# One-token attention with a cached K and V: K scored on TensorE from a transposed layout, V multiplied and summed in one VectorE pass

## The chip, the cores and the metric

The kernel runs on one NeuronCore of one Trainium2 chip. A core has five engines with a program each: TensorE for matmuls (PE in the profile, its weight loads PEld), VectorE (DVE), ScalarE (ACT), GpSimd (POOL) and SyncE (SP). They meet through semaphores. Data comes from HBM into SBUF (128 partitions) by 16 DMA engines; a transfer is issued from an engine's queue, here mostly SP's, and the transfers of one queue start in order. TensorE writes into PSUM.

The metric is the device time of one execution in microseconds (us). A profiled execution also gives the span from its first to its last instruction.

## The reference, cut to what matters

```python
B, Sq, D = 1, 1, 640                      # one token
H, Sk, Dh = 32, 8192, 192                 # 32 heads, 8192 cached positions; all float32
q = (layernorm(x) @ wq) per head
scores = einsum("bhqd,bhkd->bhqk", q, k_cache) * Dh ** -0.5
p = softmax(scores)
o = einsum("bhqk,bhkd->bhqd", p, v_cache)
h = x + o.reshape(B, Sq, H * Dh) @ wo
n = layernorm(h)
gate, up = n @ W_gate, n @ W_up           # 640 -> 1536
h2 = h + (gate * (gate > 0) * up) @ W_down
```

K and V of one head are 6.29 MB each. All heads together are 402.7 MB, `wq` and `wo` 15.7 MB each, the three FFN matrices 11.8 MB: 445.9 MB read once.

## The kernel before, in words

Every big tile lives in the pool `kv`, three slots of 128 x 12,288 floats. `load_kv` (L77) brings one head of K or V as it lies in HBM: partition p holds 64 consecutive positions of 192 numbers. All loads are issued on SP's queue; a load waits until its slot is free.

At the start the whole of `wq` comes through the same three slots, and 60 matmuls (L160) make the queries of all heads at once, 8 heads in each group of 32 partitions. `query(h)` (L168) then copies two heads' queries to all 128 partitions with one selecting matmul (L173).

The K side of a head is `head_step` (L181): DVE multiplies a quarter of the tile by the query (L188), POOL adds its upper half onto the lower (L189), and three DVE sums (L193) leave the scores as 128 x 64. `softmax_steps` (L196) takes the maximum over all scores (a DVE maximum, a TensorE transpose, a second maximum), the exponential with its sum on ACT, a matmul with ones for the total, and scales.

The V side is `values_of` (L234). Of the 64 positions of a partition, 40 go through TensorE two at a time (`pairs`, L226), 12 are scaled on ACT (L240) and 12 on DVE (L241); POOL folds the products together (L246). `finish_steps` (L289) sums over partitions with small matmuls (L299), transposes, and after each group of heads multiplies by that group's rows of `wo`, loaded by `load_wo` (L86). The last two heads use TensorE alone (`values_last`).

The loop (L325) interleaves heads: in turn h it loads K of head h+1 and V of head h, and the softmax of head h and the finishing of head h-1 are generators that `head_step(h+1)` advances between its quarters. A planner orders the rest; `keep` pins single instructions to program order.

After the loop the FFN weights come through two of the same slots (L359 to L363), `h4` takes the attention result from PSUM (L368), a layer norm follows (L370 to L386), and up, gate and down are multiplied on TensorE (L392, L409) with the residual added at L412.

Of the kernel before, what the change touches and what calls it, by code (L numbers as in the profile page):

```python
# [11 lines left out]


@with_exitstack
def kernel(
# [3 lines left out]
    kc: bass.AP,  # L19
    vc: bass.AP,  # L20
    wq: bass.AP,
    wo: bass.AP,
# [6 lines left out]
    P, Q, NQ = 128, 32, 4  # L29
    _, H, S, DH = kc.shape  # L30
    D = wq.shape[0]
    F = w_gate.shape[1]
    DJ = D // P
    R = 32
    NCH = S // (P * R)
    NS = S // P
    SUB = 16
    TW = R * DH
    HPQ = H // NQ
    QB = 512  # L40
    NQB = HPQ * DH // QB
    DG = D // NQ
    FG = F // NQ
    FJ = F // P
    SCALE = DH ** -0.5
    EPS = 1e-5
    GROUPS = [list(range(4 * i, 4 * i + 4)) for i in range(7)] + [[28, 29], [30, 31]]
    group_of = {h: (gi, i) for gi, hs in enumerate(GROUPS) for i, h in enumerate(hs)}

    kf, vf = kc[0], vc[0]  # L50
# [3 lines left out]
    wts = ctx.enter_context(tc.tile_pool(name="wts", bufs=2))  # L54
    small = ctx.enter_context(tc.tile_pool(name="small", bufs=2))
    row = ctx.enter_context(tc.tile_pool(name="row", bufs=1))
    ps_q = ctx.enter_context(tc.tile_pool(name="ps_q", bufs=2, space=bass.MemoryType.PSUM))
    ps_x = ctx.enter_context(tc.tile_pool(name="ps_x", bufs=1, space=bass.MemoryType.PSUM))
    ps_o = ctx.enter_context(tc.tile_pool(name="ps_o", bufs=1, space=bass.MemoryType.PSUM))
    ps_s = ctx.enter_context(tc.tile_pool(name="ps_s", bufs=2, space=bass.MemoryType.PSUM))  # L60
# [3 lines left out]
    xrow = const.tile([1, D], F32, name="xrow")  # L64
    nc.scalar.dma_start(xT, x[0, 0].rearrange("(p j) -> p j", p=P))
    nc.scalar.dma_start(xrow, x[0])


    wq_v = wq.rearrange("(p j) n -> p j n", p=P)
    wq_ts = []  # L70
    for j in range(0, DJ, 2):
        n = min(2, DJ - j)
        t3 = kv.tile([P, 2 * TW], F32, name="kv_t").rearrange("p (j n) -> p j n", n=TW)[:, 0:n, :]
        nc.sync.dma_start(t3, wq_v[:, j:j + n, :])
        wq_ts += [t3[:, i, :] for i in range(n)]

    def load_kv(src, h, parts):  # L77
        t = kv.tile([P, 2 * TW], F32, name="kv_t")
        v = src[h].rearrange("(p r) d -> p (r d)", p=P)
        b = 0  # L80
        for n in parts:
            nc.sync.dma_start(t[:, b:b + n], v[:, b:b + n])  # L82
            b += n
        return t

    def load_wo(gi):  # L86
        hs = GROUPS[gi]
        j = len(hs) * DH // P
        t = wts.tile([P, j, D], F32, tag="wo_t", name="wo_t")
        r0 = hs[0] * DH  # L90
        nc.sync.dma_start(t, wo[r0:r0 + len(hs) * DH, :].rearrange("(p j) n -> p j n", p=P))
        return t

    ones = const.tile([P, P], F32, name="ones")
    nc.gpsimd.memset(ones, 1.0)
    eps = const.tile([P, 1], F32, name="eps")
# [5 lines left out]
    sel = const.tile([P, NQ, P], F32, name="sel")  # L102
    nc.gpsimd.memset(sel, 0.0)
    for g in range(NQ):
        nc.gpsimd.memset(sel[g * Q:g * Q + 1, g, :], 1.0)

    par = const.tile([P, 2, Q], F32, name="par")
    for i in range(2):
        nc.vector.reduce_sum(par[:, i, 0:1], ident.rearrange("p (g c) -> p g c", c=Q)[:, :, i], axis=AX.X)
        nc.vector.tensor_copy(par[:, i, 1:Q], par[:, i, 0:1].to_broadcast([P, Q - 1]))  # L110
# [14 lines left out]

    s1 = const.tile([P, 1], F32, name="s1")
    nc.vector.reduce_sum(s1, xT, axis=AX.X)  # L127
    pm = ps_s.tile([P, 512], F32, name="ps_small")
# [9 lines left out]
    pv = ps_s.tile([P, 512], F32, name="ps_small")  # L138
# [7 lines left out]


    acc = ps_a.tile([P, DG], F32, name="acc")
    for g in range(NQ):
        nc.tensor.matmul(acc[g * Q:(g + 1) * Q, :], ones[0:1, 0:Q], xrow[:, g * DG:(g + 1) * DG],  # L150
                         start=True, stop=False)


    qps = [ps_q.tile([P, QB], F32, tag="q", name=f"qp{b}") for b in range(2)]
    qps.append(ps_x.tile([P, QB], F32, tag="x", name="qp2"))
    for j in range(DJ):
        for b in range(NQB):
            for g in range(NQ):
                c0 = g * HPQ * DH + b * QB
                nc.tensor.matmul(qps[b][g * Q:(g + 1) * Q, :], xn[:, j:j + 1].to_broadcast([P, Q]),  # L160
                                 wq_ts[j][:, c0:c0 + QB], start=(j == 0), stop=(j == DJ - 1))
    q4 = const.tile([P, HPQ * DH], F32, name="q4")
    for b in range(NQB):
        nc.scalar.mul(q4[:, b * QB:(b + 1) * QB], qps[b], SCALE)  # L164

    pair_of = {}

    def query(h):  # L168

        g, i = divmod(h, HPQ)  # L170
        if i % 2 == 0:
            q = ps_q.tile([P, QB], F32, tag="q", name="q")
            nc.tensor.matmul(q[:, 0:2 * DH], sel[:, g, :], q4[:, i * DH:(i + 2) * DH], start=True, stop=True)  # L173
            pair_of[h // 2] = q
        return pair_of[h // 2][:, (i % 2) * DH:(i % 2 + 1) * DH]
# [166 lines left out]
    for _ in done:  # L342
        pass
# [97 lines left out]
```

## Time and profile before

| | |
|---|---|
| median of 3 runs | 1044.49 us (1044.29 to 1044.98) |
| profiled execution | span 1042.8 us, 5875 instructions |
| moved by DMA | 446.28 MB, mean 428 GB/s |
| mean granted TensorE clock | 0.621 |
| TensorE clock by slice | between 0.5 and 0.9 |

How to read it: the profile lists for each engine its busy time and its share of the span; for groups of instructions (source line, engine, operation, shapes, count) the busy time of the group, the mean time of one in ns, and the idle time in front of them with what ended most of it. `SPq` or `ACTq` is an engine's sequencer, which issues transfers. The chain is the work that ended last, followed back from the last instruction. In the timeline the first two numbers are start and length in us, and a row can merge several like instructions (`x24`); for a float32 matmul two passes are recorded, so `x24` with four column groups are three steps of the sum. In the view by stretches the columns are length, busy time and count of PE, PEld, DVE, ACT and POOL, then the granted TensorE clock as a share, the share of the DMA engines, and GB/s.

### The profile page before, as it was taken

Reading aid. Unit: us, or ns where it says so; the run is one execution under the profiler, and the core shown is the slowest. Engines: PE = TensorE matmul, PEld = TensorE weight load, DVE = VectorE, ACT = ScalarE, POOL = GpSimd, SP = SyncE. Lnnn points to the kernel's source line nnn. Section 1 sums busy time; section 2 is a strip of 40 time slices with the busy share of each in tenths; the row PEclk is TensorE's granted clock in tenths of the full one; section 3 lists DMA queues with packets and bytes.
Section 4 is the critical chain, followed back from the end, with each engine's and each line's share of the span. In section 5 each row is a group of like instructions: output and inputs, shape, how many; then the busy total and the mean of one; then the engine's idle time right before and its main releaser. Section 6 shows DMA issues by size and latency. Waiting matters only on the chain.

```text
span 1042.8 us, 5875 instructions
## 1 busy us (share of the span) xinstructions
PE 311.4 (30%) x2056; PEld 91.5 (9%) x2056; DVE 779.6 (75%) x445; ACT 161.8 (16%) x471; POOL 776.5 (74%) x321
## 2 busy tenths in 40 slices
PE   1603232222234212232322222242222323230376
PEld 0100000000000000000000000000000000010122
DVE  1087988688888888688986888788886889878641
ACT  0101111011111101111110111111111111110110
POOL 0057888788887888688897888868886888888730
PEclk9955655665656556566666656565565665565577
DMA  9999999999999999999999999999999999999997
GB/s 392 446 430 432 425 441 426 437 427 436 432 434 430 428 438 424 439 425 440 432 432 430 434 432 430 433 432 434 430 423 441 436 432 430 432 436 424 433 423 307
DMA packets 12998, 446.28 MB, mean 428 GB/s; under 512 B 1573, under 2 KB 1577, under 8 KB 3114
## 3 DMA queue, kind: packets, MB, share of 16 engines
q1 hardware_dynamic: 12824, 445.92, 99.3%
q8 instruction: 16, 0.26, 0.1%
q14 instruction: 12, 0.10, 0.0%
q10 hardware_dynamic: 146, 0.01, 0.0%
HBM read 445.91 MB, written 0.00 MB: 428 GB/s over the span
## 4 chain that ended last, share of the span: by engine, by line
DMA 77%; DVE 14%; PE 5%; POOL 3%; issue 1%; ACT 0%; SPq 0%; ACTq 0%; POOLq 0%; DVEq 0%
DMA kv_t<-in_A_k_cache_dram 70%; DVE kv_t L188 12%; DMA ffn_b<-in_B_W_down_dram 3%; PE ps_small L299 2%; DMA kv_t<-in_A_v_cache_dram 2%; DMA xrow<-in_A_x_dram 2%; POOL kv_t L246 2%; PE ps_small L200 1%; POOL kv_t L189 1%; DVE sc L193 1%; PE qp L160 1%; DVE kv_t L241 1%; DVE mp L198 0%; PE pd L409 0%; SPq L82 0%
## 5 line engine op out<-in xcount | busy, mean ns | idle before, releaser
L188 DVE TENSOR_TENSOR kv_t<-kv_t,q 128x3072 f32<-128x3072 f32 x128 | 427.4, 3342 | 182.8 <-DMA kv_t<-in_A_k_cache_dram 182.4
L189 POOL TENSOR_TENSOR kv_t<-kv_t 128x1536 f32<-128x1536 f32 x128 | 438.2, 3448 | 96.1 <-DVE kv_t L188 85.1
L246 POOL TENSOR_TENSOR kv_t<-kv_t 128x1152 f32<-128x1152 f32 (+1 forms) x180 | 337.2, 1874 | 125.7 <-DVE kv_t L241 80.7
L193 DVE TENSOR_REDUCE sc<-kv_t 128x16 f32<-128x1536 f32 (+1 forms) x96 | 213.2, 2273 | 0.7 <-POOL kv_t L189 0.7
L230 PE MATMUL po<-kv_t,pn 128*2 128x384 f32 x1328 | 162.0, 653 | 104.1 <-DMA kv_t<-in_A_v_cache_dram 104.1
L200 PE MATMUL ps_small<-ident,mp 128*128 128x128 f32 x32 | 14.2, 444 | 449.0 <-DVE mp L198 449.0
L240 ACT ACTIVATE kv_t<-kv_t,pn 128x192 f32<-128x192 f32 x360 | 127.8, 441 | 101.9 <-DMA kv_t<-in_A_v_cache_dram 98.4
L241 DVE TENSOR_TENSOR kv_t<-kv_t,pn 128x2304 f32<-128x2304 f32 x30 | 103.3, 3444 | 0.0
L206 ACT ACTIVATE p<-sc,m 128x64 f32<-128x64 f32 x32 | 11.1, 348 | 583.7 <-DVE m L203 583.7
L230 PEld LDWEIGHTS po<-kv_t,pn 128*2 128x2 f32 x1328 | 38.1, 103 | 219.1 <-issue 219.1
L200 PEld LDWEIGHTS ps_small<-ident,mp 128*128 128x128 f32 x32 | 5.8, 180 | 471.7 <-issue 426.9
L276 PE MATMUL acc<-wo_t,oT 128*3 128x480 f32 x112 | 32.8, 898 | 18.0 <-DVE oT L303 18.0
L173 PE MATMUL q<-q,sel 128*128 128x384 f32 x32 | 20.7, 747 | 56.9 <-DVE kv_t L188 56.9
L208 PE MATMUL ps_small<-rs,ones 128*128 128x1 f32 x64 | 18.6, 359 | 59.7 <-ACT p L206 59.7
L213 ACT ACTIVATE pn<-p,rl 128x64 f32<-128x64 f32 x32 | 11.1, 348 | 102.7 <-DVE rl L212 102.7
L299 PE MATMUL ps_small<-kv_t,ones 128*32 128x192 f32 (+1 forms) x64 | 24.8, 508 | 2.2 <-POOL kv_t L246 2.2
L208 PEld LDWEIGHTS ps_small<-rs,ones 128*128 128x128 f32 x64 | 15.8, 307 | 86.2 <-ACT p L206 74.5
L303 DVE STREAM_TRANSPOSE oT<-ps_small 32x192 f32<-32x192 f32 (+1 forms) x32 | 11.7, 364 | 10.2 <-PE ps_small L299 9.5
L160 PE MATMUL qp<-kv_t,xn 128*32 128x512 f32 x120 | 17.2, 737 | 5.5 <-DMA kv_t<-in_A_wq_dram 3.1
L242 DVE TENSOR_TENSOR kv_t<-po,par 128x384 f32<-128x384 f32 x30 | 16.3, 544 | 0.0
L268 DVE MEMSET acc<- 128x512 f32 x1 | 0.5, 485 | 20.9 <-ACT q L164 20.9
L127 DVE TENSOR_REDUCE s<-xT 128x1 f32<-128x5 f32 x1 | 0.2, 157 | 17.1 <-DMA xT<-in_A_x_dram 17.1
(82 smaller groups left out, 102.7 us busy)
## 6 DMA issues: line engine op xcount, KB each, us to landing
kv_t<-in_A_k_cache_dram SPq DMA_DIRECT2D x32, 6144.0 KB, 24.1
kv_t<-in_A_v_cache_dram SPq DMA_DIRECT2D x31, 6144.0 KB, 23.2
wo_t<-in_A_wo_dram SPq DMA_DIRECT2D x7, 1920.0 KB, 27.1
kv_t<-in_A_wq_dram SPq DMA_DIRECT2D x2, 6144.0 KB, 17.8
ffn_a<-in_B_W_up_dram SPq DMA_DIRECT2D x1, 3840.0 KB
kv_t<-in_A_wq_dram SPq DMA_DIRECT2D x1, 3072.0 KB, 40.0
kv_t<-in_A_v_cache_dram SPq DMA_DIRECT2D x1, 3072.0 KB, 17.2
kv_t<-in_A_v_cache_dram SPq DMA_DIRECT2D x4, 768.0 KB, 20.8
```

Source lines behind the costliest of these rows:

```text
L160: nc.tensor.matmul(qps[b][g * Q:(g + 1) * Q, :], xn[:, j:j + 1].to_broadcast([P, Q]), wq_ts[j][:, c0:c0 + QB], start=(j == 0), stop=(j == ...
L188: keep(nc.vector.tensor_mul(ks, ks, q[:, None, :].to_broadcast([P, SUB, DH])))
L189: nc.gpsimd.tensor_add(ks[:, :, 0:HD], ks[:, :, 0:HD], ks[:, :, HD:DH])
L193: keep(nc.vector.reduce_sum(sc[:, i0:i1], k3[:, i0:i1, 0:HD], axis=AX.X))
L200: keep(nc.tensor.transpose(pt[:, 0:P], mp.to_broadcast([P, P]), ident))
L208: nc.tensor.matmul(pl[:, 0:1], ones, rs, start=True, stop=True)
L230: nc.tensor.matmul(po[g * Q:g * Q + 2, :], pn[:, 2 * i:2 * i + 2], vt[:, 2 * i * DH:(2 * i + 2) * DH], start=(i < NQ), stop=(i >= n - NQ))
L240: nc.scalar.activation(v3[:, r, :], v3[:, r, :], AF.Copy, scale=pn[:, r:r + 1])
L241: keep(nc.vector.tensor_mul(v3[:, RV:NS, :], v3[:, RV:NS, :], pn[:, RV:NS, None].to_broadcast([P, RN, DH])))
L246: nc.gpsimd.tensor_add(v3[:, r:r + n, :], v3[:, r:r + n, :], v3[:, s:s + n, :])
L276: nc.tensor.matmul(acc3[g * Q:g * Q + 3, 0:W3], oT[:, t:t + 3, 0], w3[:, g * W3:(g + 1) * W3], start=(gi == 0 and t == 0), stop=(gi == LAS ...
L299: nc.tensor.matmul(pt[q0:q0 + Q, 0:W], par[:, k, :] if n > 1 else ones[:, 0:Q], ob[:, k * DH + u * W:k * DH + (u + 1) * W], start=(k == 0) ...
```

## The change

The host now packs two arrays, one row of 128 x 13,248 floats for each head. In `kq` K is transposed, so that the 192 dimensions of a head run over partitions: 128 of them in columns 0 to 8,191, the other 64 in two halves in the next 4,096; behind them lie that head's columns of `wq`, 960 floats a partition. In `vo` V is transposed as well: partition 16 g + c holds, for position group g, the dimensions c, c + 16, ..., each as 1,024 consecutive positions; behind them lie that head's rows of `wo`. Two loads serve one head, and the pool `kv` has three slots of 128 x 13,248.

For each head `query` makes the query from the tile's own `wq` columns, five matmuls that leave it on all 128 partitions. `columns` turns it into columns over partitions (two short DVE multiply-and-sums with an identity, two ACT scalings with masks). `scores` is 24 matmuls of 512 columns into a 128 x 1,024 PSUM tile, where a group of 16 partitions carries the same 1,024 scores, followed by the softmax on that tile. `values` is 12 DVE passes over 128 x 1,024, each multiplying a slice of V by the probabilities and summing along the row into one column, then a matmul that adds the position groups, and two short sums that divide by the softmax total. `output` adds the head's product with `wo` to `acc` with three matmuls.

The kernel runs in the written order on each engine (`manual_schedule`): query of the next head stands between values and output of this one on TensorE. POOL only fills constants. The last V tile comes in four pieces. `x` in columns moves from ACT's queue to the front of SP's; `h4` is read from PSUM in four pieces of 32 partitions; the first two loads of `W_down` are joined. The layer norms and the FFN are as before.

```diff
-    def head_step(q, kt, *works):
-        sc = small.tile([P, NS], F32, name="sc")
-        k3 = kt.rearrange("p (r d) -> p r d", d=DH)
-        parts = [(i0, k3[:, i0:i0 + SUB, :]) for i0 in range(0, NS, SUB)]
-        for i0, ks in parts:
-            keep(nc.vector.tensor_mul(ks, ks, q[:, None, :].to_broadcast([P, SUB, DH])))
-            nc.gpsimd.tensor_add(ks[:, :, 0:HD], ks[:, :, 0:HD], ks[:, :, HD:DH])
...
+    ctx.enter_context(tc.manual_schedule())
+    xT = const.tile([P, DJ], F32, name="xT")
+    nc.sync.dma_start(xT, x[0, 0].rearrange("(p j) -> p j", p=P))
+    def load(src, parts):
+        t = kv.tile([P, TW], F32, name="kv_t")
+        b = 0
         for n in parts:
+            nc.sync.dma_start(t[:, b:b + n], src[:, b:b + n])
             b += n
         return t
+    tiles = [load(kq[0], [TW]), load(vo[0], [TW]), load(kq[1], [TW])]
...
+    def ttr(dst, a, b, scale, out):
+        nc.vector.tensor_tensor_reduce(out=out, in0=a, in1=b, scale=scale, scalar=0.0,
+                                       op0=ALU.mult, op1=ALU.add, accum_out=dst)
+    def query(kt):
+        wq = kt[:, KW:TW].rearrange("p (j n) -> p j n", n=DH)
+        pq = ps_q.tile([P, QB], F32, name="pq")
+        for j in range(DJ):
+            nc.tensor.matmul(pq[:, 0:DH], xn[:, j:j + 1].to_broadcast([P, P]), wq[:, j, :],
+                             start=(j == 0), stop=(j == DJ - 1))
+        return pq
+    def columns(pq):
...
+        ttr(q[:, 0:1], ident, pq[:, 0:D1], SCALE, junk[:, 0:D1])
+        ttr(q[:, 1:2], low, pq[:, D1:DH], SCALE, junk[:, D1:DH])
...
+        nc.scalar.mul(qs[:, 0:2, :], pk[:, 0:2, :], q[:, 0:1])
+        nc.scalar.mul(qs[:, 2, :], pk[:, 2, :], q[:, 1:2])
+        return qs
+    def scores(qs, kt):
+        sp = ps_s.tile([P, SG], F32, name="sp")
+        for u in range(0, SG, QB):
+            for i in range(3):
+                for g in range(NQ):
+                    c0 = (2 * g + i) * SG + u if i < 2 else S + g * SG + u
+                    nc.tensor.matmul(sp[g * Q:(g + 1) * Q, u:u + QB], qs[:, i, :], kt[:, c0:c0 + QB],
+                                     start=(i == 0), stop=(i == 2))
         mp = small.tile([P, 1], F32, name="mp")
+        nc.vector.reduce_max(mp, sp, axis=AX.X)
...
+        nc.tensor.transpose(pt[:, 0:P], mp.to_broadcast([P, P]), ident)
...
+        nc.vector.reduce_max(m1, pt[:, 0:P], axis=AX.X, negate=True)
+        p = pp.tile([P, SG], F32, name="p")
         rs = small.tile([P, 1], F32, name="rs")
+        nc.scalar.activation(p, sp, AF.Exp, bias=m1, accum_out=rs)
...
+        nc.tensor.matmul(pl[:, 0:1], share, rs, start=True, stop=True)
         rl = small.tile([P, 1], F32, name="rl")
+        nc.vector.reciprocal(rl, pl[:, 0:1])
+        return p, rl
+    def values(vt, p, rl):
+        op = small.tile([P, NJ], F32, name="op")
+        for j in range(NJ):
+            b = vt[:, j * SG:(j + 1) * SG]
+            ttr(op[:, j:j + 1], b, p, 1.0, b)
+        po = ps_m.tile([P, QB], F32, name="ps_small")
+        nc.tensor.matmul(po[:, 0:NJ], same.rearrange("p a c -> p (a c)"), op, start=True, stop=True)
...
+        ttr(o[:, 0:1], blk, po[:, 0:NG], rl, junk[:, 0:NG])
+        ttr(o[:, 1:2], blk2, po[:, NG:NJ], rl, junk[:, NG:NJ])
+        o2 = small.tile([P, P], F32, name="o2")
+        nc.scalar.mul(o2, side.rearrange("p a c -> p (a c)"), o[:, 1:2])
+        return o, o2
+    def output(o, o2, vt, last):
+        for i in range(2):
+            nc.tensor.matmul(acc[i * D2:(i + 1) * D2, :], o[:, 0:1].to_broadcast([P, D2]),
+                             vt[:, KW + i * HN:KW + (i + 1) * HN], start=False, stop=False, skip_group_check=True)
+        nc.tensor.matmul(acc, o2, vt[:, KW + D:TW], start=False, stop=last, skip_group_check=True)
+    kt, vt = tiles[0:2]
+    pq = query(kt)
     for h in range(H):
+        p, rl = scores(columns(pq), kt)
+        o, o2 = values(vt, p, rl)
+        done = vt
         if h + 1 < H:
+            kt = tiles[2] if h == 0 else load(kq[h + 1], [TW])
+            vt = load(vo[h + 1], [TW] if h + 2 < H else [3 * SG] * 3 + [3 * SG + WW])
+            pq = query(kt)
+        output(o, o2, done, h == H - 1)
     sqd = row.tile([1, 1], F32, name="sqd")
+    nc.scalar.activation(sqd, eps[0:1, :], AF.Sqrt)
...
-    for j0, j1 in ((0, 3), (3, 6), (6, 9), (9, 10), (10, 11), (11, 12)):
+    for j0, j1 in ((0, 6), (6, 9), (9, 10), (10, 11), (11, 12)):
...
-    nc.scalar.activation(h4, acc, AF.Copy, accum_out=hs1)
+    for g in range(NQ):
+        s = slice(g * Q, (g + 1) * Q)
+        nc.scalar.activation(h4[s], acc[s, (g % 2) * DG:(g % 2 + 1) * DG], AF.Copy, accum_out=hs1[s])
```

More of the change, by code (lines that the diff above doesn't have):

```diff
@@ L63 @@
     xT = const.tile([P, DJ], F32, name="xT")
[L64 to L75, printed above, removed]
@@ L145 @@
     nc.vector.tensor_scalar_mul(xn, xc, rstd)
[L148 to L175, printed above, removed]
@@ L196, in softmax_steps @@
-    def softmax_steps(sc, res):
+    HN = D // 2
+    acc = ps_a.tile([P, HN], F32, name="acc")
+    for i in range(2):
+        nc.tensor.matmul(acc[i * D2:(i + 1) * D2, :], ones[0:1, 0:D2], xrow[:, i * HN:(i + 1) * HN],
+                         start=True, stop=False, skip_group_check=True)
+    def ttr(dst, a, b, scale, out):
+        nc.vector.tensor_tensor_reduce(out=out, in0=a, in1=b, scale=scale, scalar=0.0,
+                                       op0=ALU.mult, op1=ALU.add, accum_out=dst)
@@ L205, in softmax_steps @@
+        p = pp.tile([P, SG], F32, name="p")
         rs = small.tile([P, 1], F32, name="rs")
-        nc.scalar.activation(p, sc, AF.Exp, bias=m1, accum_out=rs)
-        pl = ps_s.tile([P, 512], F32, name="ps_small")
-        nc.tensor.matmul(pl[:, 0:1], ones, rs, start=True, stop=True)
-        yield
-        pn = small.tile([P, NS], F32, name="pn")
-        rl = small.tile([P, 1], F32, name="rl")
-        keep(nc.vector.reciprocal(rl, pl[:, 0:1]))
-        nc.scalar.mul(pn, p, rl)
-        res += [pn]
```

272 lines of the change are left out of this document (84 added, 188 removed).

## The prediction

> **What bounds the kernel now.** I read the page's busy shares and queues first, then the chain that ended last, then single stretches of the timeline.
>
> ```profile
> PE 311.4 (30%) x2056; PEld 91.5 (9%) x2056; DVE 779.6 (75%) x445; ACT 161.8 (16%) x471; POOL 776.5 (74%) x321
> ...
> q1 hardware_dynamic: 12824, 445.92, 99.3%
> ...
> DMA 77%; DVE 14%; PE 5%; POOL 3%; issue 1%; ACT 0%; SPq 0%; ACTq 0%; POOLq 0%; DVEq 0%
> ...
> kv_t<-in_A_k_cache_dram SPq DMA_DIRECT2D x32, 6144.0 KB, 24.1
> ...
> kv_t<-in_A_wq_dram SPq DMA_DIRECT2D x2, 6144.0 KB, 17.8
> ```
>
> The transfers of one queue fill 99.3% of the span and 77% of the chain. No compute engine is above 75%. DVE's 14% of the chain are slots being freed: a K tile lands 24.1 us after its issue (last column) though its bytes take 14.6 us at the rate below, so issues run some 9 us ahead and the queue never empties.
>
> ```profile
> 56.36 13.15 DVE kv_t L188 x4
> ...
> 981.42 3.35 DVE kv_t L188
> ...
> 986.95 20.08 DMA kv_t<-in_A_v_cache_dram
> 1007.05 29.09 DMA ffn_b<-in_B_W_down_dram
> 1036.17 3.47 PE pd L409 x48
> 1039.67 0.38 DVE o L412
> ```
>
> These are rows of the chain in order of time (start, length). The first K tile is taken up at 56.36 and the last at 981.42. Between them come 31 K tiles, 30 V tiles and all of wo: 61 x 6.29 + 15.73 = 399.5 MB in 925.1 us, 431.9 GB/s. At the end the FFN weights are still landing when everything before them is done: the last projection waits for them at 1036.17, and the span closes 3.2 us after its matmuls.
>
> **The stream after the change.** The bytes are the same, 445.9 MB; wq and wo merely ride inside the tiles, which grow from 6.29 to 6.78 MB (128 x 13,248 floats). A tile then takes 15.7 us at 431.9 GB/s, a head's pair 31.4 us.
>
> ```profile
> 0.74 0.41 ACTq L65 DMA_DIRECT2D xT<-in_A_x_dram  x1
> 0.75 1.33 SPq L74 DMA_DIRECT2D kv_t<-in_A_wq_dram  x3
> ```
>
> xT moves from ACT's queue to the front of SP's, so the first tile is issued 0.41 us later, at about 1.2. The first 6.29 MB tile took 17.8 us to land, 3.2 above its 14.6 at the rate; so K0 lands at 1.2 + 3.2 + 15.7 = 20.1, and K31, 62 tiles later, at 20.1 + 62 x 15.7 = 994. Call that T. It assumes that no slot is late. K of head h+2 goes into V's slot of head h, which output(h) frees; output(h) now stands behind query(h+1) on PE, which waits for the K tile. That frees the slot some 5 us after K of h+1 lands, while V of h+1 has 15.7 us to fly: the queue stays fed with 10 us to spare. So the removed work (L188 and L193 on DVE, L189 and L246 on POOL, L240 on ACT, the wq product at the start) gains nothing: it all lay under the stream. If the stream stopped covering it, nothing of the old work would come back, only the new chain would show. What counts is whether the new serial work of one head fits in 31.4 us, and what remains of it behind T.
>
> **One head's chain.** Before, head h+1's scores were interleaved with head h's values. Now the program order on PE and DVE is one chain: query, scores, softmax, values, the small matmul po, and only then the next query. Nothing of two heads overlaps but output and columns.
>
> PE first. The scores have L160's shapes: a pass of 512 columns, four column groups side by side, two passes for fp32.
>
> ```profile
> 25.49 13.09 PE L160 MATMUL qp<-kv_t,xn 128*32 128x512 f32 x96 [2.34 <-DVE par L109]
> ...
> 29.76 0.20 PEld L160 LDWEIGHTS qp<-kv_t,xn 128*32 128x32 f32 x4 [0.66 <-issue]
> 30.62 0.18 PEld L160 LDWEIGHTS qp<-kv_t,xn 128*32 128x32 f32 x4 [0.66 <-issue]
> 31.11 0.12 PEld L160 LDWEIGHTS qp<-kv_t,xn 128*32 128x32 f32 x4 [0.31 <-issue]
> 31.54 0.12 PEld L160 LDWEIGHTS qp<-kv_t,xn 128*32 128x32 f32 x4 [0.31 <-issue]
> ```
> ```profile
> 203.60:208.20 4.60, 4.56 (x15) 0.99 (x18) 4.58 (x3) 0.39 (x2) 4.04 (x2) 0.50 1.04 449
> 208.30:214.60 6.30, 4.75 (x48) 1.24 (x42) 6.30 (x3) 3.71 (x11) 5.64 (x2) 1.00 0.95 408
> ```
>
> A pass takes 0.86 us at first and 0.43 us some 5 us later; the two windows show the granted clock going from 0.50 to 1.00 inside another burst. After 15 us of values PE starts slow each time. Query is 5 matmuls x 2 passes x 192 columns, output 2 x 2 x 320 (its first two matmuls use different column halves), scores 6 x 2 x 512: 9,344 columns, 15.6 us slow or 7.8 us fast. With 5.1 us slow: 5.1 + 10.5/2 + 0.4 for weight loads and the last pass = 10.8 us (9.6 if it speeds up at 3 us, 16 if never). The DVE and ACT steps of columns (two short sums, two scalings of about 0.3 us) run beside output's 2.1 us.
>
> Softmax, from the last head's rows:
>
> ```profile
> 1002.01 0.22 DVE L198 TENSOR_REDUCE mp<-sc 128x1 f32<-128x64 f32 x1
> ...
> 1003.33 0.32 PE L200 MATMUL ps_small<-ident,mp 128*128 128x128 f32 x1
> ...
> 1003.69 0.29 DVE L203 TENSOR_REDUCE m<-ps_small 128x1 f32<-128x128 f32 x1 [1.46 <-PE ps_small L200]
> ...
> 1004.02 0.35 ACT L206 ACTIVATE p<-sc,m 128x64 f32<-128x64 f32 x1
> 1004.27 0.19 ACT L206 ACTIVATION_READ_ACCUMULATOR p<-sc,m 128x1 f32 x1
> 1004.51 0.30 PEld L208 LDWEIGHTS ps_small<-rs,ones 128*128 128x128 f32 x2 [1.05 <-ACT p L206]
> ...
> 1004.93 0.17 DVE L212 RECIPROCAL rl<-ps_small 128x1 f32<-128x1 f32 x1 [0.95 <-PE ps_small L208]
> ```
> ```profile
> 45.02 0.60 ACT L164 ACTIVATE q<-qp 128x512 f32<-128x512 f32 x1 [0.70 <-PE qp L160]
> ```
>
> It took 3.1 us, about 1.0 of it PE being busy with other matmuls. The maximum over 1,024 instead of 64 adds 1.0 us (0.22 us for 64, and 1.04 ns an element by the rows below), the exponential 0.7 (L164's 512 take 0.60): 3.9 us.
>
> Values: twelve passes over 1,024, each multiplying two SBUF operands and summing.
>
> ```profile
> L241 DVE TENSOR_TENSOR kv_t<-kv_t,pn x30: 2540/3460/3755, 96.0 to 970.2; 128x2304 f32<-128x2304 f32 x30
> ```
> ```profile
> 96.03 2.54 DVE L241 TENSOR_TENSOR kv_t<-kv_t,pn 128x2304 f32<-128x2304 f32 x1
> ...
> 98.71 11.51 POOL L246 TENSOR_TENSOR kv_t<-kv_t 128x1152 f32<-128x1152 f32 x6 [5.58 <-DVE kv_t L241]
> ```
>
> L241 has two such operands (duration min/median/max). Its fastest, 2.54 us, is the one beside which POOL was idle for 5.58 us; POOL is idle throughout the new loop, so I take that: 1.04 ns an element plus a start. Back to back a start costs 0.07 us (the four of L188 above: 13.15 less 3.34, by three, less 3,072 x 1.04 ns). So 1.07 + 0.07. The sum's read-out is a second instruction, never seen here on DVE; between nothing and ACT's 0.19 us, and I take 0.07, another short start. 1.21 us x 12 = 14.5 us (13.7 to 16). The summing form itself is unseen too; its upper bounds are rivals below.
>
> With po at 0.7 us the chain is 10.8 + 3.9 + 14.5 + 0.7 = 29.9 us, 1.5 us below the stream's 31.4. So the stream still sets the pace, narrowly.
>
> **The end.** Here cover is missing. Before, half the work on the last V tile was spread over PE passes that followed its pieces. Now values(31) can't start before the softmax of a K tile that lands only 15.7 us earlier.
>
> ```profile
> 1015.25 1.02 PE L319 MATMUL acc<-wo_t,oT 64*32 64x160 f32 x24 [0.40 <-DVE oT L303]
> 1016.34 0.30 ACT L368 ACTIVATE h<-acc 128x160 f32<-128x160 f32 x1 [2.07 <-PE acc L319]
> ...
> 1018.30 0.56 PE L382 MATMUL ps_small<-hs,ones 128*128 128x1 f32 x2 [1.13 <-DVE hs L380]
> ...
> 1019.93 5.43 PE L392 MATMUL pu<-ffn_a,hc 128*32 128x384 f32 x40 [1.07 <-DMA ffn_a<-in_B_W_up_dram]
> ...
> 1025.44 2.14 PE L392 MATMUL pg<-ffn_a,hc 128*32 128x384 f32 x24
> ...
> 1030.78 0.56 DVE L402 SCALAR_TENSOR_TENSOR gu<-pg,us 128x384 f32<-128x384 f32 x1 [10.56 <-PE pg L392]
> 1031.37 0.84 DVE L404 STREAM_TRANSPOSE guT<-gu 128x384 f32<-128x384 f32 x1
> 1032.27 1.02 PE L409 MATMUL pd<-ffn_b,guT 128*32 128x160 f32 x24 [1.64 <-DVE guT L404]
> ```
>
> From T: PE 10.8, softmax 3.9, values 14.5 (V31's last quarter lands at T + 15.7, three passes need it, so it doesn't hold), po and the two short sums 1.1, output 2.4: attention ends at T + 32.7. h4 is now four ACT pieces with a read-out each, 0.4 us a pair as at L368: 1.7 us. The norm up to L382's end took 2.1 us: T + 36.5. Up 5.4, gate 3.5 (ten passes at 2.14 for six), gu and its transpose 1.5, down 3.4 (1.02 for six of 24 passes), then 3.2 to the close: T + 53.5. By then the weights have long landed: 18.6 MB behind T are 43 us. The moved Sqrt table load lies under output's matmuls.
>
> 994 + 53.5 = 1047.5 us of span against 1042.8; the profiled execution stands 1.7 us below the median of the runs, 1044.49, so I predict **1049.2 us**, 0.45% slower. Bounds: T 991 to 995, PE -1.2 to +0.7, values -0.8 to +1.5, the down projection +3 if PE is slow again (L409 above, 3.47 us for twelve passes): 1045 to 1053 for this case, 66%.
>
> **Rivals.**
> - *The loop outlasts the stream*, 16%. The margin is 1.5 us, gone when a pass of values takes 1.33 us instead of 1.21, or PE speeds up late. Each us of period above 31.4 costs 32 us. At 32.5 us: 1085. At L241's median, 1.50 ns an element, a pass is 1.61 and the period 34.9: 20.1 + 31 x 34.9 + 58.5 + 1.7 = 1162. For it: nothing overlaps. Against: POOL is idle.
> - *The summing multiply takes two cycles an element*, 9%. Then 2.28 us a pass, a period of 42.7 and 20.1 + 31 x 42.7 + 66.3 + 1.7 = 1412 us. Against it speaks L241's 2.54 us, but that one doesn't sum. The Trainium skill (Vector Engine (DVE) Microarchitecture Reference, Points that are easy to get wrong) says that the scalar-tensor-tensor form with two SBUF sources that aren't bf16 runs at half throughput, since no port is left for the accumulator. By that rule the time is this rival's, by the trace's row the forecast's; no run shows yet whether it holds for this instruction.
> - *The tail stays hidden: not slower*, 5%. If the path behind T were under 47 us (PE fast at once, shorter passes), the weights would decide as before, T + 43 for all bytes, less 2.3 for the last three 0.33 MB rows of W_down, plus the 6.7 us from 1036.1 to the close before: 994 + 47.4 = 1041.4 of span, 1043.1. It needs 6 us off a sum whose low ends give 2.
> - *Faster*, 4%: the same hidden tail, and the stream, now of equal large tiles, lands K31 by 991: 1040.
>
> **How the numbers follow.** 0.2% is 2 us, about what a measurement of this kernel can tell. Slower 0.91 (66 + 16 + 9), same 0.05, faster 0.04. The range is 1045 to 1095: above it lie the half-rate case and the upper part of the slow loop (14%), below it some 6%.
>
> **What would show it.** Right: q1's share near 98.5%, DVE passes of 1.2 us, DVE idle before columns waiting on K tiles, and a chain whose last 50 us hold values, output and the FFN matmuls with no weights waited for. Wrong: SP waiting long for slots and DVE busy or PE-bound without DMA waits (the loop), passes near 2.3 us (half rate), or a chain that ends on W_down (hidden).

## The result and the profile after

The changed kernel takes 1055.64 us (median of four runs, 1054.82 to 1056.03), the kernel before beside it 1044.45 (1044.29 to 1044.98). The ratio is 1.0107, with a 95% interval of 1.0092 to 1.0121. So it is slower, as forecast, but by 11.2 us where the forecast was 4.7. The measured time lies inside the forecast range, 1045 to 1095, but only because that range was drawn wide for a loop that outlasts the stream; it lies above the 1045 to 1053 that was given for the case that came.

The page of the changed kernel; its busy line, its queues, the shares of the chain and the two rows of a values pass:

```profile
span 1053.7 us, 6515 instructions
...
PE 406.9 (39%) x2396; PEld 205.3 (19%) x2396; DVE 530.3 (50%) x1154; ACT 76.6 (7%) x175; POOL 1.3 (0%) x12
...
q1 hardware_dynamic: 10952, 445.92, 98.3%
q8 instruction: 19, 0.31, 0.1%
q14 instruction: 12, 0.10, 0.0%
...
DMA 77%; PE 19%; DVE 3%; issue 0%; ACT 0%; another core or an unknown queue 0%; SPq 0%; DVEq 0%; ACTq 0%
...
L143 DVE CUSTOM_DVE_ANT_0 kv_t<-kv_t,p 128x1024 f32<-128x1024 f32 x384 | 442.6, 1222 | 30.1 <-DMA kv_t<-in_vo_dram 30.1
...
L143 DVE DVE_READ_ACCUMULATOR2_ANT op<- 128x1 f32 x384 | 32.0, 83 | 0.0
```

POOL has nothing left to do and DVE only half its time, yet the transfers fill the span as they did before: removing that work gained nothing, as it lay under the stream. DVE's instructions, though, have gone from 445 to 1,154, because every multiply-and-sum is two of them (the last two rows). That number matters below. The queues q8 and q14, named "instruction", carry blocks of the engines' programs over the same 16 DMA engines as the data. Their number alone has hardly changed; the kernel before had

```profile
q8 instruction: 16, 0.26, 0.1%
q14 instruction: 12, 0.10, 0.0%
```

but there DVE, ACT and POOL had 445, 471 and 321 instructions, and now they have 1,154, 175 and 12.

The chain of the changed kernel behind the last K tile (start, length):

```profile
1000.17 3.57 PE pq L150 x10
...
1005.29 5.33 PE sp L171 x48
1010.64 1.24 DVE mp L174
...
1014.50 1.23 DVE kv_t L143
1015.73 1.14 DVE kv_t L143
...
1027.19 1.14 DVE kv_t L143
...
1028.39 0.62 PE ps_small L194 x2
...
1029.32 1.34 PE acc L205 x4
1030.66 1.38 PE acc L207 x2
1032.06 0.39 ACT h L244 x2
...
1036.28 5.96 PE pu L268 x40
1042.25 3.28 PE pg L268 x40
...
1047.11 3.51 PE ps_small L285 x96
1050.65 0.38 DVE o L288
```

From K31 being taken up (1000.17) to the close (1053.7) there is no wait for a transfer, and it takes 53.5 us: just the length forecast. Of the 6.5 us that the forecast is short, 6.2 lie ahead of it: K31 was to be there at 994. The timeline shows how it comes late; these are the queries of five heads in a row, with PE's wait for the K tile in brackets:

```profile
272.87 3.57 PE L150 MATMUL pq<-kv_t,xn 128*128 128x192 f32 x10 [1.09 <-DMA kv_t<-in_kq_dram]
305.15 3.57 PE L150 MATMUL pq<-kv_t,xn 128*128 128x192 f32 x10 [2.01 <-DMA kv_t<-in_kq_dram]
336.49 3.57 PE L150 MATMUL pq<-kv_t,xn 128*128 128x192 f32 x10 [1.05 <-DMA kv_t<-in_kq_dram]
367.83 3.57 PE L150 MATMUL pq<-kv_t,xn 128*128 128x192 f32 x10 [1.05 <-DMA kv_t<-in_kq_dram]
400.13 3.40 PE L150 MATMUL pq<-kv_t,xn 128*128 128x192 f32 x10 [2.07 <-DMA kv_t<-in_kq_dram]
```

The heads are 31.33 us apart, but the intervals to 305.15 and to 400.13 are 32.28 and 32.30, and the wait is 1 us longer there. Nine of the 31 intervals are like that; 9 x 0.95 = 8.6 us. The trace's records of single DMA packets say what else happens in these nine:

```
8,192-byte instruction block at   43   168   294   389   515   610   736   831   958 us
long interval ends at           52.6 178.9 305.2 400.1 526.4 621.3 747.6 842.6 968.8 us
```

An ordinary row of 52,992 bytes takes 1.958 us, and 16 of them are 31.33: the steady pace is one DMA engine working through its 8 rows of a K and of a V tile without a gap. A block takes 0.33 us itself and the row behind it 2.62. The records don't name the DMA engine; rebuilt from packets that follow each other without a gap, all nine blocks lie on the same one (one record is missing near 723 us; behind it the chain is taken up again at the engine that is latest). The other three blocks on q14 lie on other engines and lengthen no interval. In the kernel before, as far as its packets can be followed (to 899 us), no DMA engine has more than four blocks of q14. A tile has landed when all 16 have their rows in, so this one sets the time, and nothing lets it catch up: near 178 us it is 1.1 us behind the others with its part of a tile, near 968 us 5.8. At the end fourteen of the others have their last weights by 1037.3, one by 1038.3 and this one at 1043.1.

**Theory A**, then: DVE's program is fetched 8,192 bytes (128 instructions) at a time, always by the same DMA engine, at about 1 us each, and that is what moved K31; beside it stands the serial end. **Rivals**: B, the longer rows stream slower in themselves; C, DVE's two-source passes hinder the writes into SBUF; D, chance delays; E, instruction fetches slow the stream as a whole, whichever engine they are for.

### The profile page after: what moved, and what is told of

The parts are those of the page before. It is cut to its first block, busy times and chain, and to the rows that moved or that the text cites. A ratio compares the mean times of both kernels' runs of the same rounds, so it can differ in the third digit from the quotient of the medians.

```text
span 1053.7 us, 6515 instructions
## 1 busy us (share of the span) xinstructions
PE 406.9 (39%) x2396; PEld 205.3 (19%) x2396; DVE 530.3 (50%) x1154; ACT 76.6 (7%) x175; POOL 1.3 (0%) x12
## 4 chain that ended last, share of the span: by engine, by line
DMA 77%; PE 19%; DVE 3%; issue 0%; ACT 0%; another core or an unknown queue 0%; SPq 0%; DVEq 0%; ACTq 0%
DMA kv_t<-in_kq_dram 74%; PE pq L150 10%; PE acc L205 3%; DMA kv_t<-in_vo_dram 3%; PE acc L207 3%; DVE kv_t L143 3%; PE pu L268 1%; PE sp L171 1%; PE ps_small L285 0%; PE pg L268 0%; ACT h L244 0%; DVE mp L174 0%; PE ps_small L194 0%; ACT p L181 0%
## 5 line engine op out<-in xcount | busy, mean ns | idle before, releaser
L143 DVE CUSTOM_DVE_ANT_0 kv_t<-kv_t,p 128x1024 f32<-128x1024 f32 x384 | 442.6, 1222 | 30.1 <-DMA kv_t<-in_vo_dram 30.1
L171 PE MATMUL sp<-kv_t,qs 128*32 128x512 f32 x1536 | 171.4, 594 | 0.8 <-ACT qs L161 0.8
L174 DVE TENSOR_REDUCE mp<-sp 128x1 f32<-128x1024 f32 x32 | 39.2, 1225 | 219.5 <-PE sp L171 219.5
L150 PE MATMUL pq<-kv_t,xn 128*128 128x192 f32 x320 | 113.5, 541 | 55.1 <-DMA kv_t<-in_kq_dram 55.1
L150 PEld LDWEIGHTS pq<-kv_t,xn 128*128 128x128 f32 x320 | 98.0, 332 | 59.2 <-DMA kv_t<-in_kq_dram 44.7
L171 PEld LDWEIGHTS sp<-kv_t,qs 128*32 128x32 f32 x1536 | 46.6, 110 | 113.8 <-issue 108.6
L181 ACT ACTIVATE p<-sp,m 128x1024 f32<-128x1024 f32 x32 | 35.7, 1115 | 266.5 <-DVE m L178 266.5
L205 PE MATMUL acc<-kv_t,o 128*64 128x320 f32 x128 | 37.1, 672 | 0.3 <-DVE o L143 0.3
L207 PE MATMUL acc<-kv_t,o 128*128 128x320 f32 x64 | 32.5, 595 | 0.0
L143 DVE DVE_READ_ACCUMULATOR2_ANT op<- 128x1 f32 x384 | 32.0, 83 | 0.0
L161 ACT ACTIVATE qs<-pick,q 128x64 f32<-128x64 f32 x32 | 11.2, 350 | 153.6 <-DVE q L143 153.6
L183 PEld LDWEIGHTS ps_small<-rs,share 128*128 128x128 f32 x64 | 10.5, 207 | 59.8 <-ACT p L181 59.8
```

What stands on the lines that cost most here:

```text
L143: nc.vector.tensor_tensor_reduce(out=out, in0=a, in1=b, scale=scale, scalar=0.0, op0=ALU.mult, op1=ALU.add, accum_out=dst)
L150: nc.tensor.matmul(pq[:, 0:DH], xn[:, j:j + 1].to_broadcast([P, P]), wq[:, j, :], start=(j == 0), stop=(j == DJ - 1))
L161: nc.scalar.mul(qs[:, 0:2, :], pk[:, 0:2, :], q[:, 0:1])
L171: nc.tensor.matmul(sp[g * Q:(g + 1) * Q, u:u + QB], qs[:, i, :], kt[:, c0:c0 + QB], start=(i == 0), stop=(i == 2))
L174: nc.vector.reduce_max(mp, sp, axis=AX.X)
L181: nc.scalar.activation(p, sp, AF.Exp, bias=m1, accum_out=rs)
```

## The experiments

**1. More DVE instructions, same work.** 36 one-element memsets a head, put where DVE waits for the scores:

```diff
+        pad = small.tile([P, 1], F32, name="pad")
+        for _ in range(36):
+            nc.vector.memset(pad, 0.0)
         mp = small.tile([P, 1], F32, name="mp")
```

> The changed kernel with 36 one-element memsets more per head on DVE, put where DVE waits for the scores (some 2 us of a 5 us gap). DVE then has 2,306 instructions instead of 1,154. Theory A (the changed kernel's DVE instructions are fetched in blocks of 8,192 bytes, 128 instructions each, always by the same one of the 16 DMA engines, 0.95 us of its time a block, and a tile has landed only when the slowest engine has its rows in): 18 blocks instead of 9, K31 taken up 8 to 9 us later than in the changed kernel, at about 1009 instead of 1000.2, and the time 8 to 9 us longer, about 1064. Rival B (the longer rows of the packed tiles stream slower in themselves) and rival C (the two-source passes on DVE get in the way of the DMA writes): nothing moves, K31 at 1000.2, 1055.6 us.

Measured: 1065.77 us, 10.1 more than the changed kernel. The page and the last K tile:

```profile
PE 402.9 (38%) x2396; PEld 204.4 (19%) x2396; DVE 596.5 (56%) x2306; ACT 76.4 (7%) x175; POOL 1.3 (0%) x12
...
q14 instruction: 21, 0.17, 0.0%
```
```profile
1010.19 3.57 PE L150 MATMUL pq<-kv_t,xn 128*128 128x192 f32 x10 [2.08 <-DMA kv_t<-in_kq_dram]
```

Nine blocks more (21 for 12) and K31 10.0 us later, 1.1 us a block. The loads and the passes are the same, so B and C can't explain it. Nor did the memsets lengthen the chain of a head: PE still waits at least 1.03 us for every K tile (1.04 in the changed kernel). The four runs lie within 1064.43 to 1066.63 us, so it isn't chance (D).

**2. As many instructions more on POOL.**

```diff
         ttr(q[:, 1:2], low, pq[:, D1:DH], SCALE, junk[:, D1:DH])
+        pad = small.tile([P, 1], F32, name="pad")
+        for _ in range(36):
+            nc.gpsimd.tensor_copy(pad, q[:, 0:1])
```

> The changed kernel with 36 one-element copies more per head on POOL, behind the head's query sums. As many instructions more as in the run beside it, on another engine. Theory A: POOL's blocks go through another DMA engine than DVE's, whose nine remain the longest delay: K31 at 1000 to 1001, time 1055 to 1057. If instruction fetches slow the stream as a whole, or POOL's blocks go through DVE's DMA engine: K31 8 to 9 us later, about 1064. B and C: 1055.6.

```profile
q14 instruction: 22, 0.18, 0.0%
```
```profile
999.43 3.52 PE L150 MATMUL pq<-kv_t,xn 128*128 128x192 f32 x10 [1.11 <-DMA kv_t<-in_kq_dram]
```

Measured: 1054.91 us. Ten blocks more, and K31 is no later (999.43), which rules out E. In the rebuilt packet chains (unbroken to 785 us) POOL's blocks lie on other DMA engines than DVE's. So a block costs nothing where it falls on a DMA engine that isn't the last one; what counts is the longest pile on one of them.

**3. The same bytes in fewer DVE instructions.**

```diff
-        for j in range(NJ):
-            b = vt[:, j * SG:(j + 1) * SG]
-            ttr(op[:, j:j + 1], b, p, 1.0, b)
+        b = vt[:, 0:KW].rearrange("p (j s) -> p j s", s=SG)
+        nc.vector.tensor_mul(b, b, p[:, None, :].to_broadcast([P, NJ, SG]))
+        nc.vector.tensor_copy(op, b[:, :, 0])
```

> The changed kernel with the twelve multiply-and-sum passes of a head replaced by one multiply over all twelve (12,288 elements, some 12.7 us against 13.85) and a copy of twelve products; the sum over the products is left out. DVE reads and writes the same bytes with 450 instructions instead of 1,154. Theory A: 3 blocks on DVE's DMA engine instead of 9, K31 at 994 to 995 instead of 1000.2; behind it the one multiply must wait for all of V31, so the rest stays within 1 us: about 1050. Rivals B and C: K31 stays at 1000.2, about 1056.

```profile
PE 405.8 (39%) x2396; PEld 204.8 (20%) x2396; DVE 507.5 (48%) x450; ACT 76.4 (7%) x175; POOL 1.3 (0%) x12
...
q14 instruction: 7, 0.06, 0.0%
```
```profile
994.75 3.57 PE L150 MATMUL pq<-kv_t,xn 128*128 128x192 f32 x10 [1.77 <-DMA kv_t<-in_kq_dram]
```

Measured: 1050.62 us, 5.0 less. DVE is nearly as busy as it was (507.5 us for 530.3), reading and writing the same tiles, and K31 stands at 994.75, 5.4 us earlier with 5 blocks fewer. Theory A holds in both directions. The packets of this kernel can be followed all the way to K31: DVE's four blocks lie on one DMA engine, and PE's are spread over eight, at most three on each.

**4. The end made shorter.** Only three passes in the last head:

```diff
-    def values(vt, p, rl):
+    def values(vt, p, rl, last):
...
-        for j in range(NJ):
+        for j in range(NJ if not last else 3):
             b = vt[:, j * SG:(j + 1) * SG]
             ttr(op[:, j:j + 1], b, p, 1.0, b)
+        if last:
+            for j in range(3, NJ, 3):
+                nc.vector.tensor_copy(op[:, j:j + 3], vt[:, j * SG:j * SG + 3])
...
```

> The changed kernel with three instead of twelve multiply-and-sum passes in the last head; nine columns of its sums are left out and filled with values copied from V31. If the changed kernel's end is the serial work behind K31, then with 10 us of it gone the last FFN weights decide: they land at 1043.1 as in the changed kernel, and from there to the close it is 4 (only the last row's matmuls left) to 6.7 us (as before): a span of 1047 to 1050, 1049 to 1051.6 us. If the weights decide already, or the clock or the FFN stage stretches, 1055.

The chain that ended last, in this kernel:

```profile
1011.90 26.87 DMA ffn_b<-in_w_down_dram
1038.77 0.14 issue
1038.90 5.28 PE ps_small L288 x96
1044.19 0.02 issue
1044.21 0.38 DVE o L291
```

Measured: 1049.00 us, 6.6 less. PE now waits for W_down, as it did before the change. So the serial end is a second cost, of its own.

**5. K one head ahead.** The loop in another order, so that the last tile to land is not followed by scores:

```diff
-    tiles = [load(kq[0], [TW]), load(vo[0], [TW]), load(kq[1], [TW])]
+    tiles = [load(kq[0], [TW]), load(kq[1], [TW]), load(vo[0], [TW])]
...
+    pn = scores(columns(query(kts[0])), kts[0])
+    kts[2] = load(kq[2], [TW])
     for h in range(H):
-        p, rl = scores(columns(pq), kt)
-        o, o2 = values(vt, p, rl)
...
+        p, rl = pn
         if h + 1 < H:
+            pn = scores(columns(query(kts[h + 1])), kts[h + 1])
+            vts[h + 1] = load(vo[h + 1], [TW] if h + 2 < H else [3 * SG] * 3 + [3 * SG + WW])
+        o, o2 = values(vts[h], p, rl)
+        output(o, o2, vts[h], h == H - 1)
+        if h + 3 < H:
+            kts[h + 3] = load(kq[h + 3], [TW])
```

> The changed kernel's parts in another order: K tiles are loaded one head ahead (K0, K1, V0, K2, V1, ... K31, V30, V31) and the scores and softmax of head h+1 stand ahead of the values of head h. Bytes and instructions are the same. If the time that the changed kernel loses at its end is the serial work behind K31 (53.5 us against some 47 that the weights need to land and be used), the weights decide the end: they land at 1043.1 in the changed kernel, and before took 6.7 us from there to the close, so a span of 1049.8 and 1051.7 us. If the end is not what costs, 1055.6. Theory A expects no change in the stream: 9 blocks, W_down's last bytes at 1043 as in the changed kernel.

Measured: 1055.22 us, no gain: the expectation was wrong. The timeline shows the first pass on V30, the first on V31 and what follows the last:

```profile
999.77 1.23 DVE L143 CUSTOM_DVE_ANT_0 kv_t<-kv_t,p 128x1024 f32<-128x1024 f32 x1 [1.35 <-DMA kv_t<-in_vo_dram]
...
1014.59 1.22 DVE L143 CUSTOM_DVE_ANT_0 kv_t<-kv_t,p 128x1024 f32<-128x1024 f32 x1
...
1028.48 0.60 PE L194 MATMUL ps_small<-op,same 128*128 128x12 f32 x2 [11.19 <-DVE op L143]
```

I had counted V31's passes and forgotten that V30 lands only one tile earlier. Two heads' passes, 28.7 us from V30's landing, replace scores, softmax and one head's passes (28.2 us in the changed kernel), one serial end for another.

**6. V30 in pieces as well**, its passes put between the scores and the softmax of head 31 (six before the maximum, three behind the exponential). `sums` hands out the passes of a V tile in portions; the lines that call it for V30 alone are left out here:

```diff
-    def scores(qs, kt):
+    def scores(qs, kt, beside=lambda n: None):
...
+        beside(6)
         mp = small.tile([P, 1], F32, name="mp")
...
         nc.scalar.activation(p, sp, AF.Exp, bias=m1, accum_out=rs)
+        beside(3)
...
-            vts[h + 1] = load(vo[h + 1], [TW] if h + 2 < H else [3 * SG] * 3 + [3 * SG + WW])
...
+                pn = scores(columns(query(kts[h + 1])), kts[h + 1], some)
+            vts[h + 1] = load(vo[h + 1], [TW] if h + 3 < H else [3 * SG] * 3 + [3 * SG + WW])
```

> K one head ahead again, and the one V tile before the last now lands in four pieces too, its passes standing between the scores and the softmax of the last head on DVE. In the run before, the end was two heads' passes back to back behind V30 (999.8 to 1028.3), which is as long as the serial work behind K31 in the changed kernel. Here V30's passes begin about 11 us earlier, at the first piece. If that was what kept the end, V31's passes end 3.5 us behind its landing, at about 1019.5, the FFN is ready for W_down at about 1041, and the weights decide (1043.1 and 4 to 6.7 us): 1049 to 1051.6 us. Otherwise 1055. By theory A the stream itself, with 9 blocks on DVE's DMA engine, stays as it is.

```profile
1015.74 28.55 DMA ffn_b<-in_w_down_dram
...
1044.34 0.52 PE ps_small L302 x8
...
1044.88 0.38 DVE o L305
```

Measured: 1049.76 us, 5.9 less than the changed kernel, with the whole computation done, and still some 5 us behind the kernel before. The chain now waits for W_down's last row, of which eight small matmuls are left. Its last bytes land at 1043.8, no earlier than the changed kernel's: the stream is still late.

**7. Both costs off.** Experiment 6, with the single multiply of experiment 3 in the heads 0 to 29:

```diff
+    def shared(vt, p):
+        op = small.tile([P, NJ], F32, name="op")
+        b = vt[:, 0:KW].rearrange("p (j s) -> p j s", s=SG)
+        nc.vector.tensor_mul(b, b, p[:, None, :].to_broadcast([P, NJ, SG]))
+        nc.vector.tensor_copy(op, b[:, :, 0])
+        return op
...
-        if h + 2 != H:
+        if h + 2 < H:
+            op = shared(vts[h], p)
+        elif h + 1 == H:
             op, some = sums(vts[h], p)
-        some(NJ)
+        if h + 2 >= H:
+            some(NJ)
```

> K one head ahead with V30 in pieces, and one multiply in place of the twelve passes in the heads 0 to 29 (their sums are left out): the exposed end and most of DVE's instructions are gone together. DVE has some 490 instructions, 3 or 4 blocks instead of 9. If the two costs are separate and are all that the change lost, the one multiply takes off again what it took off the changed kernel's end (5.0 us of time, 4.7 us of W_down's last bytes): W_down's last bytes at 1038.5 to 1039.5 instead of 1043.8, and 1044 to 1045.5 us, the time before. If the end of the kernel with K ahead hangs on something else, or the fetches matter only with the serial end, 1049 to 1050.

```profile
PE 408.6 (39%) x2396; PEld 205.6 (20%) x2396; DVE 508.7 (49%) x494; ACT 76.4 (7%) x175; POOL 1.3 (0%) x12
...
q14 instruction: 7, 0.06, 0.0%
```

Measured: 1044.74 us, beside 1044.49 for the kernel before; ratio 1.0001, interval 0.9992 to 1.0011. W_down's last bytes land at 1038.5. The serial end alone is worth 5.9 us (experiment 6), the instructions alone 5.0 (experiment 3), both together 10.9: they add up, and the 0.3 us left of the 11.2 are within what these runs can tell. What remains is the stream, with or without the change. This kernel leaves out the sums of 30 heads, so it explains the time and is no replacement.

**8 and 9. Trying to keep the sums.** A version that computes everything and still has few DVE instructions would use this. The first attempt lets ACT sum six of the twelve columns and DVE reduce the other six:

```diff
...
+            nc.vector.tensor_mul(b[:, i:i + n], b[:, i:i + n], p[:, None, :].to_broadcast([P, n, SG]))
+        for j in range(NA):
+            nc.scalar.activation(b[:, j], b[:, j], AF.Copy, accum_out=op[:, j:j + 1])
+        nc.vector.reduce_sum(op[:, NA:NJ], b[:, NA:NJ], axis=AX.X)
...
```

> As the run beside it, and in the first 30 heads each multiply-and-sum pass is replaced: two multiplies over six columns each on DVE, six sums on ACT and one reduction over the other six on DVE. DVE has some 540 instructions (4 blocks of 8,192 bytes) instead of 1,154 (9), ACT some 550 (4 blocks) instead of 175. Theory A: ACT's blocks go through another DMA engine than DVE's, so the longest delay falls from 9 blocks to 4 or 5, W_down's last bytes land 3.8 to 4.8 us earlier than in the run beside it, and the time is as much shorter: 1045 to 1047.5 us. Rivals B and C (row length, DVE's traffic): no change, or, as DVE and ACT now move more bytes in SBUF, later. V20's first 1,152 columns come in three slices of 120 and 8, 88 and 40, and 104 and 24 rows, to see which of the 16 DMA engines carries DVE's blocks; they move less than 0.5 us of any engine's share.

Measured: 1185.60 us, far from the 1045 to 1047.5 expected. In program order the next head's query stands behind these sums on DVE and PE, and the chain of a head is 36.5 us long, above the stream's 31.3. One head of it, by windows (length; busy PE, PEld, DVE, ACT, POOL; granted clock, DMA share, GB/s):

```profile
506.77:543.28 36.51, 12.42 (x69) 6.42 (x69) 22.02 (x14) 8.52 (x17) 0.00 (x0) 0.64 0.88 372
```

372 GB/s: this is the forecast's first rival, the loop that outlasts the stream, made on purpose by 5 us more DVE time. The slices in V20 tell nothing here, as the DMA engines run empty between tiles.

The second attempt takes query, columns and scores of a later head in beside the passes, and gives seven columns to ACT; its edit is long and not shown.

> The sums shared with ACT again (seven of a head's twelve columns, DVE reduces five), but K's query, columns and scores now stand beside the values of the head two before, so that the longer DVE part (some 19 us) no longer stands in one chain with them; in the run before, that chain was 36 us a head and outlasted the stream. Longest delay by theory A: DVE about 520 instructions, ACT about 600, 4 to 5 blocks each on DMA engines of their own, against 9. So W_down's last bytes land at 1039 to 1040 instead of 1043.8, and the time is 1045 to 1046.5 us against 1049.8 with K one head ahead. Rivals B and C: 1049.8. If the chain of a head still outlasts 31.3 us, far above 1050. Three slices of V24 by 120 and 8, 88 and 40, 104 and 24 rows, as before.

Measured: 1057.42 us (1053.94 to 1060.02), where 1045 to 1046.5 was expected. The loop no longer holds the stream up; PE waits 17 us for a K tile on average, and DVE has 524 instructions, ACT 595. Yet K31 is taken up at 991.20, where the changed loop of experiment 6 has 985.70. Some 4.4 us of that are the slices (next paragraph); the 4 to 5 us that fewer blocks should have saved are gone as well. Intervals between K tiles are up to 2 us too long where no block is fetched, and a row of 52,992 bytes takes 1.978 us on average over all of them, where it is 1.966 in the changed kernel. ACT reads and writes 28 KB of each row again here, so rival C may be at work in this kernel; that was not tested alone and stays open.

**10. Which DMA engine?** The first 1,152 columns of V24 in slices by rows:

```diff
...
-            vt = load(vo[h + 1], [TW] if h + 2 < H else [3 * SG] * 3 + [3 * SG + WW])
+            vt = load(vo[h + 1], [(256, [(0, 120), (120, 128)]), (384, [(0, 88), (88, 128)]), (512, [(0, 104), (104, 128)]), TW - 1152] if h == 23 else [TW] if h + 2 < H else [3 * SG] * 3 + [3 * SG + WW])
```

> The changed kernel, with the first 1,152 columns of V24 in three slices of 120 and 8, 88 and 40, and 104 and 24 rows (256, 384 and 512 columns), to see by which rows' absence the late DMA engine is known. Time as the changed kernel, 1055 to 1057 us, K31 at 1000 to 1001.

Measured, in one run: 1059.87 us, K31 at 1004.58, 4.4 later. The slices mixed the order of the packets so much that the engines couldn't be told apart, and the two intervals around V24 are 2.9 and 1.5 us too long. It answers nothing but what such slices cost.

**11. The same question at the end**, on experiment 6:

```diff
-    for j0, j1 in ((0, 6), (6, 9), (9, 10), (10, 11), (11, 12)):
+    for j0, j1, r in ((0, 6, P), (6, 9, 120), (9, 10, 88), (10, 11, 104), (11, 12, 72)):
```

(rows 0 to r and r to 128 in a DMA each)

> K one head ahead with V30 in pieces (1049.8 us), and the last six rows of W_down, 48 x 2,560 bytes on each DMA engine, each loaded in two parts by rows: 120 and 8 (three rows), 88 and 40, 104 and 24, 72 and 56. At the end only the late DMA engine still moves bytes; which of the four row splits leave it idle or loaded tells which engine it is. Theory A: the end moves with that engine's share alone. If it gets nothing of the splits that spare it, W_down's last bytes land 1 to 5 us earlier than 1043.8 and the time is as much shorter, 1045 to 1049 us; if it gets the larger shares, up to 1.5 us later, 1051. Rivals B, C and D (whole stream slow): all engines finish together, the splits by fewer engines cost 0 to 2 us, 1050 to 1052.

```profile
1015.98 0.28 SPq L257 DMA_DIRECT2D ffn_b<-in_w_down_dram  x1
1026.04 0.31 SPq L255 DMA_DIRECT2D ffn_b<-in_w_down_dram  x1
1033.68 0.30 SPq L257 DMA_DIRECT2D ffn_b<-in_w_down_dram  x1
1041.48 0.30 SPq L255 DMA_DIRECT2D ffn_b<-in_w_down_dram  x1
1047.52 0.31 SPq L257 DMA_DIRECT2D ffn_b<-in_w_down_dram  x1
```

Measured: 1058.69 us. With nine pieces instead of five SP no longer issued them in one go; the last four went out 6 to 10 us apart, so W_down's last bytes came at 1052.85 whichever engine was late. All three expectations missed it, and the engine's number stays open.

**12. The kernel before, with more DVE instructions.**

```diff
+        pad = small.tile([P, 1], F32, name="pad")
+        for _ in range(36):
+            keep(nc.vector.memset(pad, 0.0))
         keep(nc.vector.reduce_max(mp, sc, axis=AX.X))
```

> The kernel before with 36 one-element memsets more per head on DVE, ahead of the maximum; its planner shifts some of PE's small matmuls with it. DVE has 1,597 instructions instead of 445 and stays below 82% busy. Theory A, if it is no property of the changed kernel: 9 blocks more on one DMA engine, the stream's end 6 to 9 us later, 1050 to 1054 us. If the fetches' delay needs the changed kernel's tiles or passes: 1044.5 to 1046.

```profile
DMA 65%; DVE 21%; PE 7%; issue 6%; ACT 0%; SPq 0%; ACTq 0%; DVEq 0%
...
q14 instruction: 21, 0.17, 0.0%
```

Measured: 1058.85 us, ratio 1.0154 (1.0121 to 1.0187), 14.4 us slower, more than either expectation; one of the four runs took 1066.23. There are nine instruction blocks more (21 for 12), and W_down's last bytes land 11.4 us later (1049.5 for 1038.0). But this is not theory A's pile. The last packets of W_down end together here, without the break of 2.6 us that stands in the changed kernel between the last of the other engines and the late one, so no single DMA engine is behind. The memsets stand on this kernel's chain (DVE has 21% of it for 14%, 7% with the memsets alone, and DMA 65% for 77%): most likely they hold up DVE, so that slots come free later and the stream as a whole is late, which no run tests alone. Whether DVE's blocks would also cost time in the kernel before stays open.

## Why the forecast was right in direction and too small in size

- *The removed work gains nothing*: right. POOL at 0% and DVE at 50% changed nothing in the stream.
- *One head's chain fits*: right, with little room. Forecast 10.8 us for PE, 3.9, 14.5 and 0.7; measured in the last head 10.5, 3.9, 13.9 and about 1. PE waits 1.05 us for a K tile in an ordinary head, where I had 1.5 us of margin.
- *The passes*: a pass starts 1.15 us after the one before, and the read-out (83 ns) lies inside, where I had 1.21. So the summing multiply runs at the plain multiply's rate, and the rival of two cycles an element is out. The rule of the Trainium skill (Vector Engine (DVE) Microarchitecture Reference, Points that are easy to get wrong) by which it would take twice as long does not hold for this instruction: 1.15 us for 1,024 elements from two fp32 operands in SBUF, not 2.28.
- *The end, T + 53.5*: measured 53.5. That it fits to the tenth is luck: the up projection took 0.6 us longer and the passes 0.6 less, and output and the norm together 0.7 longer, which PE, the gate and po took back. The mechanism, a serial end with no weights waited for, is shown by the chain. Experiments 4 and 6 show its cost as 6.6 and 5.9 us; the forecast had 6.1 (53.5 against 47.4).
- *T = 994*: wrong, measured 1000.17, and this is the step that failed. "So K0 lands at ... 20.1, and K31, 62 tiles later, at 20.1 + 62 x 15.7 = 994." K0 was right (20.36), the undisturbed pace even a little better (15.665 a tile, 2.2 us over 62). But the step took over the pace of the kernel before, where, as far as can be followed, no DMA engine has more than four blocks of q14, and added nothing for the longer pile of instruction blocks that DVE's 1,154 instructions bring: 9 x 0.95 = 8.6 us. 994 + 0.3 - 2.2 + 8.6 = 1000.7, within 0.6 of what was measured. My bounds for T, 991 to 995, had no term for it, although the page of before shows q1 without a gap and names the instruction queues.
- *The rivals*: the loop didn't outlast the stream; the tail was not hidden.

## What to carry to other kernels

When transfers fill the span, count the instructions as well as the bytes: the programs come over the same DMA engines, and in this kernel the engine with many small instructions delays one of the 16, for which every tile waits. Fewer DVE instructions brought the time back (experiments 3 and 7), faster ones would not. How to keep the sums and save the instructions is not shown: both attempts to share them with ACT were slower. When the order of loads is changed to shorten the end, add up the work behind each of the last two or three tiles, not only behind the last.

## What the runs showed of the hardware

- DVE's program comes in blocks of 8,192 bytes, one for each 128 instructions (9 blocks more for 1,152 instructions more). By the rebuilt packet chains all of them pass one DMA engine, and each costs it 0.95 to 1.1 us, though the block itself takes 0.33; why the row behind it takes 2.62 us instead of 1.96 is open. PE's blocks have 16,384 bytes (q8: 19 in the changed kernel) and change from DMA engine to DMA engine. The Trainium skill (Runtime: NRT & Kernel Launch, Instruction fetch mechanics) calls the cost of a block boundary mostly hidden and gives 16 KiB for a block. That is the size of PE's blocks here and twice that of DVE's. For the engine that runs the program the trace agrees (the idle time ahead of the passes, 30.1 us in all, is put down to V tiles alone); for a full data stream it doesn't.
- Three slices of a tile by 120, 88 and 104 rows, with the rest of the rows in DMAs of their own, cost 4.4 us in one tile (one run), though the bytes are the same.
- With W_down in nine pieces at the end of SP's queue the last ones went out up to 10 us apart, where five had gone out in 7.2 us together.
